# Attention with relative bias, then a max-of-three MoE: transposes moved between the scores and the products with v

## The chip, the cores and the metric

The kernel runs on one core of a Trainium2 chip. The metric is the device time of one execution in microseconds (us); the time of a kernel is the median of several executions. One execution is recorded by the hardware profiler, and all rows of a profile are from that one. The engines of the core are named as in the profile: PE is TensorE (matmuls), PEld its weight loads, DVE is VectorE, ACT is ScalarE, POOL is GpSimd, SP is the engine that issues the DMAs. Each engine carries out its own instructions in the order in which the program issues them; engines wait for one another by semaphores.

## What is computed

The reference, cut to what matters. B = 4, H = 8, S = 576, D = 64; the second part has 2304 tokens, d_model 512, d_ff 768.

```python
scores = scale * np.matmul(q, k.transpose(0, 1, 3, 2))
rel = (pos[:, None] - pos[None, :]).astype(np.float32)
psi_rel = np.log1p(np.abs(rel))
psi_i = np.log1p(np.maximum(pos[:, None].astype(np.float32), 1.0))
x = (psi_rel / psi_i)[..., None]
bias = np.maximum(x @ w1 + b1, 0.0) @ w2
scores = scores + bias.transpose(2, 0, 1)[None, :, :, :]
attn = np.exp(scores - np.max(scores, axis=-1, keepdims=True))
attn = attn / (np.sum(attn, axis=-1, keepdims=True) + 1e-09)
attn_out = np.matmul(attn, v)
x = attn_out.transpose(0, 2, 1, 3).reshape(B * S, H * D)
h = np.maximum(np.maximum(x @ mw1, x @ mw2), x @ mw3)
out = h @ mw_out
```

## The kernel before

The program has three stages. A bias stage builds the bias of all heads and writes it to DRAM. The attention stage works through 16 units; a unit is one batch and two heads, and two units form a pair. The MoE stage follows on the same engines; its weights are converted in small pieces of side work that are threaded into the attention stage.

The order of work is written out by hand (a manual schedule): the program issues everything in the order of the code, and each engine follows it.

A pair takes NS = 9 steps, eight pairs make 72 steps, n = 0 to 71, and four more (72 to 75) empty the pipeline. A step handles 128 rows of scores of both heads of a unit; one step of each pair, y = MIX = 4, takes the last 64 rows of both units together. From the second pair on y = n % 9. In step n the kernel does these things, each for a different stage of the pipeline:

- scores S of step n (`front`, L258): twelve matmuls of 288 columns into two tiles `s`; in the MIX step 16 matmuls at L272. The two `s` buffers are one step's, so the next scores wait for both shifts of this step.
- products P with v (`queue_pv`, L363; matmuls at L385): a finished group of 256 or 320 columns has five products, which wait in the list `pvq`. Step n takes 3, 2, 3, 2, 3, 2, 2, 2 or 1 of them, by n % 9; in the first 18 steps 3, but never across the end of a group. The accumulator `pv` has one buffer. A finished group is copied out by VectorE (`split_x`, L403).
- shift (L283, VectorE L289): scores plus bias, and the row minimum; exponential (`expo`, L295, ScalarE L303) with its row sums; one for each of the two heads.
- normalisation of step n - 2 (`norm`, L309): a reciprocal on VectorE (L313) for every two steps, and a multiplication on GpSimd (L317).
- transposes T of step f = n - 4 (`flip`, L326; transposes at L344): 16 into two tiles `tp` of one bank each, and two into a small tile `lp`. The first transpose of a step writes `lp`. `tp` has two buffers, which one step fills; `lp` has one.
- copies of the transposes into `et`: ScalarE copies one `tp` (L431) and the first part of `lp` (L432), VectorE the other `tp` (L434). In the MIX step `lp` has two parts, for two units; the second is copied by ScalarE at the end of the step (L458). `et` has two buffers, one for each group.

On TensorE a step is S, P, T. On ScalarE it is, as a rule, exponential 0, exponential 1, copies; in steps after which a group is queued or n % 9 = 7 (`ends`) it is exponential 0, copies, exponential 1, and then the rest. On VectorE it is shift 0, shift 1, the copies of finished products, side work (`between`; in `ends` steps it comes last), the reciprocal, the copy of `tp`. A group is queued at the end of the steps n % 9 = 8, 1, 3 and 5, so its products begin in the step after. The transposes of the MIX step (f % 9 = 4) fall into n % 9 = 8.

Of the kernel before, what the change touches and what calls it, by code (L numbers as in the profile page):

```python
# [19 lines left out]
def kernel(  # L20
# [12 lines left out]
    nc = tc.nc  # L33
# [117 lines left out]
    def finish(pool, k, load, g, i, keep):  # L151
        bs = pool.tile([128, S + 16], F32, tag="bs", bufs=12 + KEPT, name=f"bs{g}")
        ip = k["ipo"][:, g:g + 1]
        w = S + 15
        o = bs[:, 0:w]
        if load["act"] + 0.96 * w + 165 <= load["dve"] + 1.04 * w + 185:
            nc.scalar.activation(o, i, ACTF.Copy, scale=ip)
            load["act"] += 0.96 * w + 165
        else:
            nc.vector.tensor_scalar(out=o, in0=i, scalar1=ip, scalar2=None, op0=ALU.mult)  # L160
            load["dve"] += 1.04 * w + 185

        def write(pair=None):

            n, step = (H, 1) if pair is None else (2, H // 2)
            dst = bass.AP(tensor=bias_d.tensor, offset=bias_d.offset + 16 * g * H * BW,
                          ap=[[H * BW + 1, 16], [step * BW, n], [1, S + 15]])
            nc.sync.dma_start(out=dst, in_=bs[::step, 0:S + 15])

        if keep:  # L170
            write(0)
            kept.append(write)
        else:
            write()
# [5 lines left out]
    def load_bias(hp, t):  # L180
        if t < NTQ:
            nc.sync.dma_start(out=bias_t[t], in_=bias_rows(128 * t, 128, hp, 0, S, 2))
        else:
            for p in (0, LEFT):
                nc.sync.dma_start(out=bias_t[t][p:p + LEFT], in_=bias_rows(LB, LEFT, hp, 0, S, 2))
# [11 lines left out]
    NS = len(STEPS)  # L197
# [3 lines left out]
    NSTEP = len(sched)  # L201
# [5 lines left out]
    def step_of(pair, y):  # L207
        return ORDERS[units[2 * pair][0] % 2][y]

    class Attention:  # L210
# [198 lines left out]
        def step(self, n, more=()):  # L409
            m, f = n - BATCH, n - LAG  # L410
            if n < NSTEP:
                pair, y = fronts[n]
                which, t = step_of(pair, y)
                un = 2 * pair + which
                if pair + 1 < PAIRS and y in (0, 5):
                    self.load_qk(2 * pair + 2 + (y == 5))
                if y in (3, 7) and (pair or y == 7):
                    self.load_v(2 * pair + (y == 7))
                self.front(n)
            back = 0 <= f < NSTEP  # L420
            for _ in range((3, 2, 3, 2, 3, 2, 2, 2, 1)[n % NS] if n >= 2 * NS else 3):
                if self.pvq and self.pvq.pop(0)() and n < 2 * NS:
                    break
            done = [(un, g) for at, un, g in ((MIX if fronts[f][0] else 3, 0, 1), (1, 0, 0), (6, 1, 1), (8, 1, 0))
                    if back and fronts[f][1] == at]
            ends = bool(done) or n % NS == 7
            rest = []

            def empty():
                tp0, tp1, left = self.flip(f)  # L430
                nc.scalar.copy(*tp0[0])  # L431
                nc.scalar.copy(*left[0])  # L432
                for x in tp1:
                    nc.vector.tensor_copy(*x)  # L434
                rest.extend(tp0[1:] + left[1:])

            def between():
                for w in more:
                    w.go(False)

            if n < NSTEP:
                for h in range(2):
                    self.shift(n, h)
                    if not (ends and h):
                        self.expo(n, h)
            self.split_x()
            if not ends:
                between()
            if 0 <= m < NSTEP:
                self.norm(m)  # L450
            if back:
                empty()
            if ends:
                if n < NSTEP:
                    self.expo(n, 1)
                between()
            for x in rest:
                nc.scalar.copy(*x)  # L458
            if n < NSTEP and units[2 * pair + 1][1] == border[-1] and which and units[2 * pair][0] + 1 < HP:
                load_bias(units[2 * pair][0] + 1, t)  # L460
            for un, g in done:
                un += 2 * fronts[f][0]
                self.queue_pv(un, g, *self.et[un])
            if n < NSTEP:
                pair, y = fronts[n]
                k = n - (NS * pair + (3 if pair else 6))
                if 0 <= k < 2 and 2 * pair + 2 < len(units):
                    if k == 0:
                        self.splits = self.prep(2 * pair + 2, None if pair else nc.vector)
                    next(self.splits)  # L470
                if pair and y <= 1:
                    if y == 0:
                        self.splits = self.prep(2 * pair + 1)
                    next(self.splits)
            for w in dict.fromkeys(more):
                if w.go(True):
                    break
# [573 lines left out]
    with tc.manual_schedule():  # L1051
# [4 lines left out]
        n = 0  # L1056
# [209 lines left out]
```

## Time and profile before

| | before |
|---|---|
| median of 3 runs | 544.99 us (544.58 to 545.15) |
| the profiled execution | 545.0 us |
| its span, first to last instruction | 543.2 us |
| TensorE busy | 526.1 us (97%), 5209 matmuls |
| VectorE busy | 441.3 us (81%) |
| ScalarE busy | 362.0 us (67%) |
| GpSimd busy | 295.8 us (54%) |
| mean granted TensorE clock | 0.997 |

The attention stage's scores begin at 48 us and its last products end at 272 us of the span. A busy time is the share in which an engine's records cover the time; the ends of matmuls are modelled, so on TensorE the starts are the safer thing to read: from the first matmul of S to the first of P, and so on. A row of the timeline gives the start, the duration of the merged group, engine, line, operation, out<-in with shapes, and in brackets the idle time of the engine ahead of it with its releaser.

### The profile page before, as it was taken

Reading aid. Unit: us, or ns where it says so; the run is one execution under the profiler, and the core shown is the slowest. Engines: PE = TensorE matmul, PEld = TensorE weight load, DVE = VectorE, ACT = ScalarE, POOL = GpSimd, SP = SyncE. Lnnn points to the kernel's source line nnn. Section 1 sums busy time; section 2 is a strip of 40 time slices with the busy share of each in tenths; the row PEclk is TensorE's granted clock in tenths of the full one; section 3 lists DMA queues with packets and bytes.
Section 4 is the critical chain, followed back from the end, with each engine's and each line's share of the span. In section 5 each row is a group of like instructions: output and inputs, shape, how many; then the busy total and the mean of one; then the engine's idle time right before and its main releaser. Section 6 shows DMA issues by size and latency. Waiting matters only on the chain.

```text
span 543.2 us, 13700 instructions
## 1 busy us (share of the span) xinstructions
PE 526.1 (97%) x5209; PEld 435.5 (80%) x5209; DVE 441.3 (81%) x915; ACT 362.0 (67%) x812; POOL 295.8 (54%) x296
## 2 busy tenths in 40 slices
PE   7999889999999999999899999999999999999997
PEld 3455666676766666667599999999999999999997
DVE  7998789999998999888598878767886357798883
ACT  7998899998989898988575542443424325454552
POOL 1957687697898987776500525656476534400000
PEclk9999899999999999999999999999999999999999
DMA  5895985664694166211101234531274520666552
GB/s 168 229 344 151 343 256 171 209 181 127 196 287 136 25 201 189 69 23 24 40 1 62 96 116 150 200 134 43 77 272 155 176 87 0 216 188 193 171 164 79
DMA packets 74034, 80.76 MB, mean 149 GB/s; under 512 B 23216, under 2 KB 54576, under 8 KB 73968
## 3 DMA queue, kind: packets, MB, share of 16 engines
q1 hardware_dynamic: 73824, 79.58, 46.7%
q8 instruction: 41, 0.67, 0.5%
q10 hardware_dynamic: 144, 0.29, 0.2%
q14 instruction: 25, 0.20, 0.1%
HBM read 50.61 MB, written 28.99 MB: 147 GB/s over the span
## 4 chain that ended last, share of the span: by engine, by line
PE 58%; DVE 2%; DMA 1%; ACT 1%; issue 1%; DVEq 0%; ACTq 0%
PE p L607 11%; PE p L605 11%; PE p L606 11%; PE pv L385 5%; PE p_o L977 3%; PE p_o L975 3%; PE p_o L976 3%; PE s L279 3%; PE tp L344 2%; PE c L605 2%; PE c L606 2%; PE c L607 2%; DMA hin<-h_d 1%; PE lp L344 1%; PE s L272 1%
## 5 line engine op out<-in xcount | busy, mean ns | idle before, releaser
L317 POOL TENSOR_SCALAR e<-e,rc 128x576 f32<-128x576 f32 x144 | 113.3, 805 | 31.5 <-DVE rc L313 24.0
L303 ACT ACTIVATE e<-sn,nm 128x576 f32<-128x576 f32 x144 | 111.7, 777 | 16.6 <-DVE nm L289 13.7
L289 DVE CUSTOM_DVE_ANT_0 sn<-s,bias 128x576 f32<-128x576 f32 x144 | 102.9, 752 | 12.1 <-PE s L279 7.6
L385 PE MATMUL pv<-et,vt 128*64 128x320 f32 (+1 forms) x496 | 74.2, 419 | 2.6 <-ACT et L431 2.0
L497 POOL TENSOR_TENSOR wl<-wr,wh 128x256 fp32r<-128x256 f32 x25 | 23.4, 963 | 74.8 <-ACT wh L693 74.8
L434 DVE COPY et<-tp 128x512 f32<-128x512 f32 x72 | 48.9, 679 | 14.4 <-PE tp L344 11.5
L344 PE MATMUL tp<-ident,e 64*128 64x64 f32 x1152 | 55.7, 227 | 0.0
L385 PEld LDWEIGHTS pv<-et,vt 128*64 128x64 f32 x496 | 31.6, 136 | 26.4 <-issue 5.6
L279 PE MATMUL s<-kh,qh 64*128 64x288 f32 x256 | 50.2, 338 | 1.8 <-DVE nm L289 1.4
L244 POOL TENSOR_TENSOR kl<-kr,kh 128x576 fp32r<-128x576 f32 x16 | 41.3, 2583 | 19.3 <-ACT kh L241 18.8
L344 PEld LDWEIGHTS lp<-ident,e 64*128 64x128 f32 x144 | 19.9, 138 | 33.3 <-issue 20.8
L431 ACT COPY et<-tp 128x512 f32<-128x512 f32 x72 | 41.4, 575 | 6.8 <-PE lp L344 6.2
L344 PEld LDWEIGHTS tp<-ident,e 64*128 64x128 f32 x1152 | 45.7, 140 | 0.0
L134 PE MATMUL bp<-hid,w2s 128*32 128x79 f32 (+51 forms) x640 | 41.0, 391 | 3.4 <-DVE hid L113 3.1
L279 PE MATMUL s<-kl,qh 64*128 64x288 f32 x256 | 43.3, 297 | 0.0
L279 PE MATMUL s<-kh,ql 64*128 64x288 f32 x256 | 42.3, 293 | 0.1
L113 DVE TENSOR_SCALAR hid<-sm,bp 128x528 f32<-128x528 f32 (+17 forms) x108 | 40.5, 454 | 0.0
L134 PEld LDWEIGHTS bp<-hid,w2s 128*32 128x32 f32 x640 | 20.4, 109 | 24.5 <-issue 15.7
L344 PE MATMUL lp<-ident,e 64*128 64x64 f32 x144 | 35.6, 248 | 2.8 <-ACT et L432 1.3
L497 POOL TENSOR_TENSOR wl<-ws,wh 128x256 fp32r<-128x256 f32 x28 | 29.4, 1074 | 14.3 <-ACT wh L695 14.3
L652 ACT COPY u<-p 128x384 f32<-128x384 f32 x24 | 11.5, 480 | 37.0 <-PE p L607 37.0
L279 PEld LDWEIGHTS s<-kh,qh 64*128 64x128 f32 x256 | 30.0, 189 | 4.8 <-DVE nm L289 3.8
(231 smaller groups left out, 1620.2 us busy)
## 6 DMA issues: line engine op xcount, KB each, us to landing
bias_d<-bs SPq DMA_DIRECT2D x36, 295.5 KB, 5.4
bias<-bias_d SPq DMA_DIRECT2D x16, 576.0 KB, 6.0
w<-in_moe_w_dram SPq DMA_DIRECT2D x36, 256.0 KB, 3.2
h_d<-ht SPq DMA_DIRECT2D x18, 384.0 KB, 3.4
hin<-h_d SPq DMA_DIRECT2D x16, 384.0 KB, 4.6
qr<-in_qd_dram SPq DMA_DIRECT2D x16, 288.0 KB, 5.1
kr<-in_kd_dram SPq DMA_DIRECT2D x16, 288.0 KB, 5.5
vt<-in_v_dram SPq DMA_DIRECT2D x32, 128.0 KB, 3.3
```

Source lines behind the costliest of these rows:

```text
L134: nc.tensor.matmul(bp[32 * c:32 * c + 32, o:o + w], lhsT=w2s, rhs=src, start=True, stop=True)
L279: nc.tensor.matmul(ss[h][:, x, 0:HALF], lhsT=u[q][p, 128 * t:128 * t + 128], rhs=u[k][p, cols], start=(j == 0), stop=(j == 2))
L289: nc.vector.tensor_tensor_reduce(out=sn.rearrange("p (a b) -> p a b", a=2), in0=st["s"][h][:, :, 0:HALF], in1=bt.rearrange("p (a b) -> p a ...
L303: nc.scalar.activation(st["e"][:, S * h:S * h + S], sn, ACTF.Exp, scale=-1.0, bias=nm, accum_out=self.sm[:, x:x + 1])
L317: nc.gpsimd.tensor_scalar(out=e, in0=e, scalar1=self.rc[:, x:x + 1], scalar2=1.0, op0=ALU.mult, op1=ALU.mult)
L344: return nc.tensor.transpose(to, e2[p, k0:k0 + 128], ident[p, p])
L385: nc.tensor.matmul(pv[p], lhsT=w, rhs=x, start=(c == 0), stop=(c == NTQ))
L434: nc.vector.tensor_copy(*x)
L497: eng.tensor_tensor(out=out, in0=f(a), in1=f(b), op=op)
L605: nc.tensor.matmul(o, lhsT=hi[:, c], rhs=h[:, j], start=first and j == 0, stop=False, **on)
L606: nc.tensor.matmul(o, lhsT=hi[:, c], rhs=l[:, j], start=False, stop=False, **on)
L607: nc.tensor.matmul(o, lhsT=lo[:, c], rhs=h[:, j], start=False, stop=last and j == 1, **on)
```

## The change

From n = 9 on, except in steps with n % 9 = 8, a step is "turned". In a turned step the copies of finished products (`split_x`) stand at its head, the transposes follow the scores, and the products follow the transposes. ScalarE is issued the copies of the transposes (all parts of `lp` with them) ahead of the exponentials. VectorE is issued the shifts, then the copy of its `tp`, then the reciprocal, then the side work. The four steps after the last scores are turned too. The first nine steps and those with n % 9 = 8 stay in the old order.

```diff
+                turned = n >= NS and n % NS != NS - 1
+                if turned:
+                    self.split_x()
                 self.front(n)
+            else:
+                turned = True
+                self.split_x()
             back = 0 <= f < NSTEP
-            for _ in range((3, 2, 3, 2, 3, 2, 2, 2, 1)[n % NS] if n >= 2 * NS else 3):
-                if self.pvq and self.pvq.pop(0)() and n < 2 * NS:
-                    break
+
+            def products():
+                for _ in range((3, 2, 3, 2, 3, 2, 2, 2, 1)[n % NS] if n >= 2 * NS else 3):
+                    if self.pvq and self.pvq.pop(0)() and n < 2 * NS:
+                        break
+
+            if not turned:
+                products()
...
             def empty():
                 tp0, tp1, left = self.flip(f)
-                nc.scalar.copy(*tp0[0])
-                nc.scalar.copy(*left[0])
+                soon = len(left) if turned else 1
+                for x in tp0 + left[:soon]:
+                    nc.scalar.copy(*x)
+                if turned:
+                    products()
+                    if n < NSTEP:
+                        for h in range(2):
+                            self.shift(n, h)
                 for x in tp1:
                     nc.vector.tensor_copy(*x)
-                rest.extend(tp0[1:] + left[1:])
+                rest.extend(left[soon:])
...
-            if n < NSTEP:
+            if turned:
+                if back:
+                    empty()
+                else:
+                    products()
+                for h in range(2 if n < NSTEP else 0):
+                    self.expo(n, h)
+                if 0 <= m < NSTEP:
+                    self.norm(m)
+                between()
+            else:
                 for h in range(2):
                     self.shift(n, h)
                     if not (ends and h):
                         self.expo(n, h)
-            self.split_x()
-            if not ends:
-                between()
-            if 0 <= m < NSTEP:
-                self.norm(m)
-            if back:
-                empty()
-            if ends:
-                if n < NSTEP:
+                self.split_x()
+                if not ends:
+                    between()
+                if 0 <= m < NSTEP:
+                    self.norm(m)
+                if back:
+                    empty()
+                if ends:
                     self.expo(n, 1)
-                between()
-            for x in rest:
-                nc.scalar.copy(*x)
+                    between()
+                for x in rest:
+                    nc.scalar.copy(*x)
```

## Rows read from the trace of the kernel before

**Rows 1.** Busy time by engine in one pair's stretch (PE, PEld, DVE, ACT, POOL).

```profile
205.00:232.00 27.00, 26.78 (x354) 18.19 (x354) 24.38 (x64) 24.56 (x66) 19.92 (x24) 1.00 0.38 115
```

**Rows 2.** Timeline, TensorE, step 54 to the scores of step 55.

```profile
204.43 0.40 PE L279 MATMUL s<-kh,qh 64*128 64x288 f32 x1
205.11 0.40 PE L279 MATMUL s<-kh,qh 64*128 64x288 f32 x1 [0.28 <-DVE nm L289]
...
206.10 1.84 PE L385 MATMUL pv<-et,vt 128*64 128x320 f32 x12
...
207.87 0.77 PE L344 MATMUL tp<-ident,e 64*128 64x64 f32 x16
...
208.44 0.38 PE L279 MATMUL s<-kh,qh 64*128 64x288 f32 x2
```

**Rows 3.** Timeline, ScalarE and VectorE, the same stretch.

```profile
204.47 0.78 ACT L303 ACTIVATE e<-sn,nm 128x576 f32<-128x576 f32 x1 [0.63 <-DVE nm L289]
...
205.38 0.67 DVE L434 COPY et<-tp 128x512 f32<-128x512 f32 x1
...
205.82 0.78 ACT L303 ACTIVATE e<-sn,nm 128x576 f32<-128x576 f32 x1
...
206.83 0.19 ACT L458 COPY et<-lp 128x64 f32<-128x64 f32 x1
```

**Rows 4.** Timeline, ScalarE and TensorE, step 8: second copy of `lp`, next transpose.

```profile
69.06 0.19 ACT L458 COPY et<-lp 128x64 f32<-128x64 f32 x1
...
69.39 0.24 PE L344 MATMUL lp<-ident,e 64*128 64x64 f32 x1 [1.01 <-ACT et L458]
```

**Rows 5.** Timeline, steps 18 and 63: first product, second copy of `lp`.

```profile
98.05 1.83 PE L385 MATMUL pv<-et,vt 128*64 128x320 f32 x12
...
98.85 0.20 ACT L458 COPY et<-lp 128x64 f32<-128x64 f32 x1
...
233.17 1.83 PE L385 MATMUL pv<-et,vt 128*64 128x320 f32 x12
...
233.66 0.21 ACT L458 COPY et<-lp 128x64 f32<-128x64 f32 x1
```

**Rows 6.** Timeline, TensorE, step 55 and step 72: products and transposes.

```profile
209.41 0.76 PE L385 MATMUL pv<-et,vt 128*64 128x320 f32 x4
...
210.64 0.27 PE L344 MATMUL lp<-ident,e 64*128 64x64 f32 x1
...
260.82 0.27 PE L344 MATMUL lp<-ident,e 64*128 64x64 f32 x1
...
261.52 0.76 PE L385 MATMUL pv<-et,vt 128*64 128x320 f32 x4
```

**Rows 7.** Timeline, TensorE, step 58 (n % 9 = 4): mixed scores, then products.

```profile
217.43 1.76 PE L272 MATMUL s<-kr,qr 64*64 64x288 f32 x16
...
217.89 0.78 PEld L272 LDWEIGHTS s<-kr,qr 64*64 64x64 f32 x14 [0.28 <-DVE nm L289]
...
219.12 0.41 PEld L385 LDWEIGHTS pv<-et,vt 128*64 128x64 f32 x6 [0.44 <-ACT et L432]
```

**Rows 8.** Timeline, steps 72 to 75: products and the second copy of `lp`.

```profile
259.05 1.84 PE L385 MATMUL pv<-et,vt 128*64 128x320 f32 x12 [0.88 <-ACT et L431]
...
260.02 0.20 ACT L458 COPY et<-lp 128x64 f32<-128x64 f32 x1
...
264.30 1.84 PE L385 MATMUL pv<-et,vt 128*64 128x320 f32 x12 [0.77 <-ACT et L431]
...
269.59 1.95 PE L385 MATMUL pvlast<-et,vt 128*64 128x256 f32 x16 [0.82 <-ACT et L432]
```

**Rows 9.** Timeline, TensorE, step 61: scores, then products.

```profile
226.35 0.78 PE L279 MATMUL s<-kh,qh 64*128 64x288 f32 x2
...
227.71 0.44 PE L385 MATMUL pv<-et,vt 128*64 128x256 f32 x2
```

**Rows 10.** Timeline, GpSimd, steps 57 and 58: normalisations, four merged.

```profile
216.11 2.91 POOL L317 TENSOR_SCALAR e<-e,rc 128x576 f32<-128x576 f32 x4 [0.83 <-DVE rc L313]
```

## Prediction

> **What bounds the kernel now.** I read first the busy shares of one stretch as long as a pair of units, then the order of time on TensorE, then on ScalarE and VectorE in the same stretch, and last who released whom. In 27 us TensorE is busy for 26.78, VectorE for 24.38, ScalarE for 24.56 [rows 1]: TensorE sets the pace of the attention stage, the others are some 10% behind. So the change can win only what TensorE waits for, and loses whatever new wait it puts in front of TensorE.
>
> One step of TensorE before is scores S, products P, transposes T. Prices by starts: S to P 0.97 (208.44 to 209.41), two products of 320 columns 1.23, three 1.76, T to the next S 0.58 [rows 2, 6]. Only T directly ahead of P stands at 0.70 (260.82 to 261.52) [rows 6], in the four steps after the last scores.
>
> The regular wait is in the first step of every pair (n % 9 = 0). Its scores start at 204.43, their second half only at 205.11, released by VectorE's shift; P starts at 206.10 [rows 2]. There are six such steps from step 18 to 63. The other regular one is n % 9 = 4 (raw scores of both units' last 64 rows): there P's weight load was idle 0.44 until ScalarE's copy of `lp` [rows 7].
>
> **The change, part by part.** No instruction is added or removed; only orders move. From n = 9 on, except n % 9 = 8, TensorE does S, T, P; ScalarE does both its copies of the transposes (`tp`, `lp`) ahead of the two exponentials; VectorE does the copies of finished products at the head of the step, then shifts, its `tp` copy, the reciprocal, the side work.
>
> *Switching on TensorE.* Before, a step holds S to P (0.97), P to T, T to S (0.58). After, it holds S to T, T to P (0.70), P to S. S to T and P to S are not shown without a wait. The shapes in the rows tell which neighbours resemble each other: S and T are both 64\*128, P is 128\*64 [rows 2]. T to S costs nothing visible (207.87 to 208.44 [rows 2], 18 transposes), so I take S to T as free too: S then lasts 0.97 less the 0.12 to 0.15 by which T to P exceeds T to S, 0.82 to 0.85, and P to S costs what P to T costs. Sum: 0.83 + 0.70 against 0.97 + 0.58, so 0 within 0.02 a step. The other end, S to T as dear as S to P, is 0.12 to 0.15 in each of 55 steps, 7 to 8 us; the row of T to S is the nearest, so I take 0. (The Trainium skill, TensorEngine Tiling (Array Packing), Key Properties, says that a change of the tiling mode, not of the tile, drains the engine; by it S to T is free and the two changes a step stay two, the sum is 0; the 0.70 against 0.58 in rows 6 agrees with it.)
>
> *The step after the one that keeps the old order (n % 9 = 0).* This is the term that decides. `lp` has one buffer. In step n % 9 = 8 the transposed step is the mixed one, with two copies out of `lp`; only the first is made at once, the second (line 458) stands last on ScalarE, behind the second exponential: the first exponential starts at 204.47, the second at 205.82, the L458 copy at 206.83, when the scores of the next step are 2.4 us old [rows 2, 3]. Before, T of that next step is behind S and three products and starts at 207.87, a full us later, so nobody waits. After, T stands directly behind S, its first transpose writes `lp`, and the products are queued behind it on TensorE. That T really waits for L458 is shown once: L458 starts at 69.06, the first transpose starts at 69.39, idle 1.01 until L458 [rows 4]. So T starts at L458 + 0.33, P at L458 + 0.33 + 0.70; before, P started at its own time and T cost 0.58 behind it. Loss a step = L458 start - P start + 0.45.
> Step 54: 206.83 - 206.10 + 0.45 = 1.18. Step 18: 98.85 - 98.05 + 0.45 = 1.25; step 63: 233.66 - 233.17 + 0.45 = 0.94 [rows 2, 3, 5]. The other three (27, 36, 45) give 0.93, 1.19, 1.17 in the same way. Six steps: 6.7 us. L458 can't come sooner: its ScalarE chain begins with VectorE's shift of step 8, which step 8 does as before. What waits behind: the products, then the next scores, and on ScalarE the exponentials of this step, which now stand behind the `tp` copy.
>
> *The steps after the last scores.* Step 71 is also n % 9 = 8, with L458 at 260.02; P started at 259.05 [rows 8]. After: T at 260.35, P at 261.05. From there, three products 1.76, T 0.70, two 1.23, T 0.70, three 1.76, T 0.70, two 1.07 (with no T behind them): 7.9, so the last products start at 269.0 against 269.59. The waits of 0.77 and 0.82 for ScalarE's copies [rows 8] are covered by T and P now in between. Gain 0.6.
>
> *n % 9 = 4.* T comes between the mixed scores and P, and the copies it needs lead ScalarE. The wait of 0.44, less some 0.16 that a change of shape leaves anyway, goes: 0.28; the rest of that step's delay is the shift (weights released at 217.89 [rows 7]) and stays. Of seven such steps five show it: gain 1.2, bounds 0 and 2.
>
> *Small waits elsewhere.* The largest lets 1.36 pass between S and P instead of 0.97 [rows 9]; some 15 of 0.06 to 0.39 sum to 3.2. They come from VectorE being late with a shift because of side work. VectorE's `tp` copy no longer waits for T behind three products, but the side work itself stays in front of the next shift. I take 1.0 gained, bounds 0 and 3.2.
>
> *GpSimd's normalisation.* T moves ahead by the length of P, so e must be normalised sooner; and the reciprocal falls behind VectorE's `tp` copy (0.61 to 0.67 [rows 3]), though ahead of the side work. For step 58 GpSimd begins at 216.11 with four, so the two that T needs end at 217.57 [rows 10]; T would start at 217.43 + 1.0 [rows 7], 0.8 later. Cover holds by about the delay; cost 0, bound 0.2 in each of some 14 tight steps, 3 us.
>
> *The first nine turned steps.* There the products are still cut in other portions (three, then the rest of a group), and a group's `et` buffer comes free only with the products of the same step, which now stand behind T. The copies of steps 11, 13 and 15 wait for them, and T of the next step for the copies: some 0.1 each beyond cover. Steps 9 and 10 give about 0.2 back. Net cost 0.2, bounds -0.5 and 1.
>
> Sum: 6.7 - 0.6 - 1.2 - 1.0 + 0.2 = +4.1. The profiled execution of before took 545.0 (span 543.2 and 1.8 around it), the median of the runs shown is 544.99, so nothing has to be rescaled: 549.1. After the attention stage TensorE is full, so the delay comes through to the end.
>
> **The rivals.**
> *Faster: T is not held by L458.* If the second small copy were no condition of the first transpose, or came sooner, T would wait for the big copies only: VectorE's begins at 205.38 and lasts 0.67 [rows 3], so P at 206.05 + 0.70 = 206.75 against 206.10, less 0.58: +0.07 a step, 0.4 in six, and the tail gains 2. Sum 0.4 - 2 - 1.2 - 1.0 + 0.2 = -3.6: 541.4. The wait in rows 4 and the copy's fixed place on ScalarE speak against it. Chance 0.09. (The Trainium skill, Perfetto Trace Analysis, Matmuls, asks that independent groups rotate through PSUM banks so that evacuation overlaps the next group; `lp` doesn't rotate, so by it the wait is there. Rows 4 agree.)
> *No change: the loss is given back.* The extra us a pair lets VectorE and ScalarE catch up, and all waits of the pair's other steps (1.2 + 0.8 of n % 9 = 4 beyond it, 3.2 small) vanish: 6.7 - 0.6 - 2 - 3.2 + 0.2 = +1.1, or with P to S cheaper by 0.02 a step 0: 545 to 546.1. Against it: side work is fixed in the order and hits VectorE after the shifts of a later step. Chance 0.12.
> *Much slower: the unseen switch or a late GpSimd.* S to T costs 0.12 in 55 steps, or T waits 0.2 for e: +3 to +7 on top: 552 to 556. T to S at 0.58 speaks against it. Chance 0.09.
>
> **How the numbers follow.** Forecast as summed, 547 to 551.3, chance 0.70. About 0.2% (1.1 us) is what a measurement of this kernel can tell from no change. The range takes in the no-change case's upper part: 545.4 to 551.6. Faster by over 0.2%: 0.10; within: 0.13; slower: 0.77.
>
> **What would show it.** In the profile after, in steps 18, 27, 36, 45, 54, 63 and 72: weight loads of `lp` idle over 1 us until ScalarE's L458 (its line will differ), T 2.2 to 3.0 after its scores, the next scores 4.5 to 5.4 after them (before 3.4 to 4.3). Waits of P for `et` gone. T in the other turned steps 0.8 to 0.9 behind S. I am wrong if T in n % 9 = 0 starts within 1.8 of its scores, if the idle time before it names GpSimd or VectorE, or if S to T stands near 0.97 in ordinary steps.

## The result and the profile after

The change makes the kernel slower: 551.16 us median (550.08 to 551.49, 4 runs) beside 545.07 (544.58 to 545.18, 4 runs) of before, a ratio of 1.011 with a 95% interval of 1.0093 to 1.0128. On another chip the same two kernels took 551.40 (5 runs) and 546.22 (15 runs), ratio 1.0099 [1.0085, 1.0112]. The profiled execution of after took 550.08, span 548.3, mean granted clock 0.999. The forecast was 549.1, range 545.4 to 551.6.

The time from the scores of one step to the next scores is read off the starts in the timeline of TensorE. These stretches add up to the difference of the two profiled executions:

| stretch | before | after | difference |
|---|---|---|---|
| start of the span to the scores of step 9 | 69.95 | 69.72 | -0.2 |
| steps 9 to 17 | 27.07 | 29.70 | +2.6 |
| steps 18 to 70 | 158.70 | 161.84 | +3.1 |
| scores of step 71 to the first MoE matmul | 16.18 | 15.76 | -0.4 |
| MoE stage | 271.3 | 271.3 | 0.0 |

The third stretch hardly varies: three more profiles of kernels with the same steps there (e2, e9 and e10 below) gave 161.82 to 161.89, and another in the old order (e4) 158.69. By kind of step (n % 9), before to after: the six of 0 together +5.7; those of 4 -1.2; those of 3 -0.9; those of 6 -0.6; those of 2 +0.3; the rest -0.2.

The first rows are those that answer [rows 1 to 3]: the busy times of a pair's stretch (the columns of [rows 1]), then step 54 on TensorE, then on ScalarE. The line numbers have moved: L444 is ScalarE's copies at the transposes (L431, L432 before), L451 is VectorE's (L434), L484 the second copy of `lp` (L458), L572 to L582 the conversions of weights, the side work. All rows are of after.

```profile
205.00:232.00 27.00, 25.91 (x355) 18.16 (x355) 22.85 (x62) 24.66 (x66) 21.80 (x24) 1.00 0.54 163
```

```profile
209.30 0.74 PE L279 MATMUL s<-kh,qh 64*128 64x288 f32 x2
...
211.70 0.24 PE L344 MATMUL lp<-ident,e 64*128 64x64 f32 x1 [1.00 <-ACT et L484]
...
212.40 1.84 PE L385 MATMUL pv<-et,vt 128*64 128x320 f32 x12
214.17 0.40 PE L279 MATMUL s<-kh,qh 64*128 64x288 f32 x2
...
215.06 0.21 PE L344 MATMUL lp<-ident,e 64*128 64x64 f32 x1
...
215.71 0.76 PE L385 MATMUL pv<-et,vt 128*64 128x320 f32 x4
...
216.94 0.40 PE L279 MATMUL s<-kh,qh 64*128 64x288 f32 x2
```

```profile
209.00 0.78 ACT L303 ACTIVATE e<-sn,nm 128x576 f32<-128x576 f32 x1 [0.24 <-DVE nm L289]
...
209.78 0.57 ACT L444 COPY et<-tp 128x512 f32<-128x512 f32 x1
210.24 0.21 ACT L444 COPY et<-lp 128x64 f32<-128x64 f32 x1
210.35 0.78 ACT L303 ACTIVATE e<-sn,nm 128x576 f32<-128x576 f32 x1
...
211.36 0.19 ACT L484 COPY et<-lp 128x64 f32<-128x64 f32 x1
```

In a pair's stretch TensorE is now busy 25.91 of 27 us where it was 26.78. The wait stands in step 54, between scores and transposes: the scores end at 210.7, the second copy of `lp` starts at 211.36 behind the second exponential, and the first transpose starts 0.34 later, at 211.70. The products follow at 212.40, three us behind the scores; before it was 1.67 [rows 2]. The step after it (scores at 214.17) is an ordinary one: transposes at +0.89, products 0.65 behind them, next scores 1.23 behind those.

One row must not be taken at its word. The weight load of that transpose names GpSimd, the matmul names ScalarE; GpSimd's own timeline decides.

```profile
211.67 0.13 PEld L344 LDWEIGHTS lp<-ident,e 64*128 64x128 f32 x1 [1.21 <-POOL e L317]
```

```profile
207.96 1.47 POOL L317 TENSOR_SCALAR e<-e,rc 128x576 f32<-128x576 f32 x2 [0.63 <-DVE rc L313]
```

GpSimd had normalised both tiles of that step by 209.43, 2.3 us before the transpose; the copy of L484 ended at 211.55.

What TensorE waited for from 60 to 280 us (the view of waits: line, releaser, total us, times, longest), after:

```profile
PE lp L344 <- ACT et L484: 7.8, 7, 2.2
PE lp L344 <- POOL e L317: 2.2, 2, 1.2
PE pv L385 <- PE lp L344: 1.3, 3, 0.7
PE lp L344 <- ACT et L444: 1.3, 2, 1.0
PE s L279 <- DVE nm L289: 0.9, 4, 0.3
```

Seven waits for L484, 7.8 us: step 8, which before has too [rows 4]; steps 18, 27, 45, 54 and 63; and the longest, 2.2, step 72. Step 36 stands in the second line, by its row on TensorE, with GpSimd's rows behind it:

```profile
156.59 0.24 PE L344 MATMUL lp<-ident,e 64*128 64x64 f32 x1 [1.01 <-POOL e L317]
```

```profile
152.82 1.48 POOL L317 TENSOR_SCALAR e<-e,rc 128x576 f32<-128x576 f32 x2 [2.74 <-DVE rc L313]
155.78 1.46 POOL L317 TENSOR_SCALAR e<-e,rc 128x576 f32<-128x576 f32 x2
```

Step 36 transposes what step 32 computed. Counted from the start of the program, the pair of multiplications at 152.82 is that of step 32, and it ended at 154.30, 2.3 us before the transpose; the pair at 155.78 belongs to the next step's transposes. L484 starts at 156.25, and the transpose 0.34 later, as in step 54. In all seven steps from 18 to 72 the first transpose starts 0.33 to 0.35 behind the start of L484, and GpSimd had ended the tiles of the step at least 1.7 us before it. The third line of the waits, products that wait although the engine named is TensorE itself, is the second finding (below). None of its five lines has products waiting for a copy into `et`, which [rows 8] showed for before.

### The profile page after: what moved, and what is told of

Read it like the earlier page. It is cut to its first block, busy times and chain, and to the rows that moved or that the text cites. A ratio compares the mean times of both kernels' runs of the same rounds, so it can differ in the third digit from the quotient of the medians.

```text
span 548.3 us, 13699 instructions
## 1 busy us (share of the span) xinstructions
PE 525.0 (96%) x5209; PEld 438.4 (80%) x5209; DVE 434.9 (79%) x915; ACT 360.8 (66%) x812; POOL 287.5 (52%) x296
## 4 chain that ended last, share of the span: by engine, by line
PE 82%; ACT 8%; DVE 4%; issue 2%; DMA 2%; POOL 1%; DVEq 0%; ACTq 0%; POOLq 0%
PE pv L385 13%; PE p L631 10%; PE p L633 10%; PE p L632 10%; PE s L279 8%; PE bp L134 7%; PE tp L344 5%; ACT e L303 4%; PE p_o L1003 3%; PE p_o L1001 3%; PE p_o L1002 3%; PE s L272 2%; PE c L631 2%; PE c L632 2%; PE c L633 2%
## 5 line engine op out<-in xcount | busy, mean ns | idle before, releaser
L451 DVE COPY et<-tp 128x512 f32<-128x512 f32 x72 | 49.2, 684 | 9.3 <-PE tp L344 4.1
L444 ACT COPY et<-tp 128x512 f32<-128x512 f32 x72 | 41.8, 580 | 21.4 <-PE lp L344 17.5
L344 PE MATMUL tp<-ident,e 64*128 64x64 f32 x1152 | 52.7, 224 | 0.0
L244 POOL TENSOR_TENSOR kl<-kr,kh 128x576 fp32r<-128x576 f32 x16 | 35.9, 2244 | 23.9 <-ACT kh L241 23.4
L344 PEld LDWEIGHTS tp<-ident,e 64*128 64x128 f32 x1152 | 47.1, 139 | 0.0
L134 PE MATMUL bp<-hid,w2s 128*32 128x79 f32 (+51 forms) x640 | 42.5, 411 | 2.8 <-DVE hid L113 1.8
L344 PE MATMUL lp<-ident,e 64*128 64x64 f32 x144 | 33.0, 229 | 11.9 <-ACT et L484 7.8
L134 PEld LDWEIGHTS bp<-hid,w2s 128*32 128x32 f32 x640 | 21.9, 115 | 24.0 <-issue 14.3
```

Source lines behind the costliest of these rows:

```text
L134: nc.tensor.matmul(bp[32 * c:32 * c + 32, o:o + w], lhsT=w2s, rhs=src, start=True, stop=True)
L344: return nc.tensor.transpose(to, e2[p, k0:k0 + 128], ident[p, p])
```

## The experiments

Three groups of kernels, each with the kernel before on the same chip; its medians there are 546.03, 545.90 and 546.22 us. Every edit is to the changed kernel unless it is said otherwise. The columns on the right are read from each kernel's one profiled execution.

| run | median us (runs) | ratio to before [95%] | steps 9 to 17 | 18 to 70 | 71 to MoE |
|---|---|---|---|---|---|
| e1_lp_early | 545.91 (12) | 1.0000 [0.9984, 1.0017] | 28.69 | 158.19 | 14.79 |
| e2_from18 | 550.71 (6) | 1.0091 [1.0069, 1.0112] | 26.85 | 161.89 | 17.34 |
| e3_both | 544.29 (10) | 0.9959 [0.9944, 0.9974] | 28.11 | 158.09 | 14.80 |
| e4_before_lp_early | 546.34 (12) | 0.9999 [0.9984, 1.0014] | 28.20 | 158.69 | 16.19 |
| e5_step0_old | 546.56 (10) | 1.0018 [0.9992, 1.0044] | 28.88 | 157.42 | 17.16 |
| e6_copies_last | 569.84 (4) | 1.0437 [1.0396, 1.0478] | 30.66 | 178.07 | 15.75 |
| e7_split_first | 543.28 (12) | 0.9951 [0.9933, 0.9969] | 27.50 | 157.25 | 14.78 |
| e8_all_turned | 543.03 (12) | 0.9947 [0.9923, 0.9972] | 28.83 | 157.25 | 14.26 |
| e9_after_again | 551.40 (5) | 1.0099 [1.0085, 1.0112] | 28.97 | 161.82 | 17.30 |
| e10_from18_again | 550.05 (5) | 1.0077 [1.0058, 1.0096] | 28.24 | 161.87 | 15.77 |
| e11_split_from9 | 543.28 (5) | 0.9946 [0.9926, 0.9966] | 29.26 | 157.25 | 14.78 |
| e12_split_again | 544.19 (11) | 0.9961 [0.9944, 0.9977] | 27.48 | 157.28 | 14.78 |

### Is it the second copy of `lp`?

e1_lp_early: in the step that keeps the old order, ScalarE copies the second part of `lp` right behind the first, ahead of the second exponential.

```diff
-                soon = len(left) if turned else 1
+                soon = len(left)
```

> The changed kernel, and in the steps n % 9 = 8 the second copy out of lp stands right behind the first, ahead of the second exponential. Theory (T of the next step waits for that copy): T at n % 9 = 0 then waits only for the big copies and starts some 1.7 us after its scores instead of 2.2 to 2.6; 0.7 to 0.8 us in each of six steps and 1.1 us in the steps after the last scores come back, 5.5 us: 545.6 us, and no idle time of TensorE names this copy any more. Rival (the copy is only the last name on a wait that the turned order makes anyway, by T ahead of P and exponentials behind copies): within 0.2% of the changed kernel, 551 us.

e4_before_lp_early is its control, the same edit to the kernel before (line 432):

```diff
-                nc.scalar.copy(*left[0])
+                for x in left:
+                    nc.scalar.copy(*x)
```

> The kernel before, with only the second copy out of lp moved ahead of the second exponential. Theory (in the old order T starts a full us after that copy, nobody waits): 545.0 us, no change within 0.2%. Rival (the late copy already cost something, and any gain of the first experiment is this gain): 543 to 544 us.

e5_step0_old leaves the copy where it is and puts the steps with n % 9 = 0 back into the old order:

```diff
-                turned = n >= NS and n % NS != NS - 1
+                turned = n >= NS and 0 < n % NS < NS - 1
```

> The changed kernel with the steps n % 9 = 0 left in the old order too, the late second copy out of lp unchanged. Theory (only T of that step meets the late copy): the step goes from 4.9 us back to 3.9, six times 5.7 us; the next step's T, turned, then meets copies of an old-order step, made behind the exponentials, and loses some 0.3 us each time: 547 us, and TensorE doesn't wait for L458's successor in steps 18 to 63. Rival (any change of order between neighbouring steps costs such a wait): 549 to 551 us.

e1, step 54 on TensorE and ScalarE:

```profile
204.89 0.74 PE L279 MATMUL s<-kh,qh 64*128 64x288 f32 x2
...
206.31 0.24 PE L344 MATMUL lp<-ident,e 64*128 64x64 f32 x1
...
207.01 1.83 PE L385 MATMUL pv<-et,vt 128*64 128x320 f32 x12
...
208.78 0.40 PE L279 MATMUL s<-kh,qh 64*128 64x288 f32 x2
```

```profile
205.84 0.32 ACT L444 COPY et<-lp 128x64 f32<-128x64 f32 x2
206.05 0.79 ACT L303 ACTIVATE e<-sn,nm 128x576 f32<-128x576 f32 x1
```

With both small copies at 205.84 the transposes start 1.42 behind the scores where after has 2.40, and the step takes 3.89 instead of 4.87. All of it goes: 18 to 70 is 3.65 shorter than in after, the tail 0.97, the time is that of before. In before the same edit changes nothing (158.69, 16.19): there nobody waits for that copy. e5 removes the wait in the six steps by the other end and 18 to 70 falls by 4.4; the step behind it then lasts 3.07 instead of 2.77, and the wait in the tail, which this edit doesn't touch, stays. By kind of step, in e1 those of n % 9 = 0 fall by 5.2 in all against after, and those of 2 rise by 1.5, which e7 takes up. So one copy out of a tile with one buffer carries the loss of the stage; the turned order without it is worth 0.5 us there and 1.4 in the tail, less than the 3.6 that the prediction's rival had put on it.

### The first nine turned steps

e2_from18 begins to turn at step 18, and e3_both has both edits.

```diff
-                turned = n >= NS and n % NS != NS - 1
+                turned = n >= 2 * NS and n % NS != NS - 1
```

> The changed kernel, turned from n = 18 on instead of n = 9. Theory (in the first turned pair the copies of T wait for the et buffer, that is for products that now stand behind T, and the next accumulator waits behind them): the stretch from the scores of step 9 to those of step 18 goes from 29.7 us back to 27.1, of which 1.1 us are waits for et and the accumulator and 1.5 us a wait of ScalarE for a weight's DMA that may or may not be there; 548.5 to 550 us. Rival (the long first pair was an accident of one execution): 551 us.

> Both edits: second copy out of lp early, and turned from n = 18 on. Theory (two separate causes, one behind the other on TensorE): the gains add up, 5.5 and 1.1 to 2.6: 543 to 544.6 us, slightly below the kernel before, since n % 9 = 4 and 3 gain some 2 us. Rival (the turned order itself is dearer than the old one): not below 547 us.

e3 is 1.6 us below e1 on the same chip, but e2, at 550.71, is hardly below after. The columns tell why: its first pair is 2 to 3 us shorter, its tail 1.6 longer, with the same instructions there; the tail has a section below. Where the first pair loses shows on TensorE, VectorE and ScalarE in steps 11 and 12 of after:

```profile
78.34 0.24 PE L344 MATMUL lp<-ident,e 64*128 64x64 f32 x1 [1.23 <-POOL e L317]
...
82.70 1.57 PE L385 MATMUL pv<-et,vt 128*64 128x320 f32 x10 [0.66 <-PE lp L344]
```

```profile
80.42 0.69 DVE L451 COPY et<-tp 128x512 f32<-128x512 f32 x1 [0.54 <-PE pv L385]
81.03 1.05 DVE L576 TENSOR_SCALAR wa<-wa 128x512 uint32<-128x512 uint32 x1
82.00 0.61 DVE L405 COPY xb<-pv 128x128 f32<-128x128 f32 x3
```

```profile
76.89 0.67 ACT L572 ACTIVATE wa<-w 128x512 f32<-128x512 f32 x1 [1.58 <-DMA vt<-in_v_dram]
77.46 0.57 ACT L444 COPY et<-tp 128x512 f32<-128x512 f32 x1
77.93 0.27 ACT L444 COPY et<-lp 128x128 f32<-128x128 f32 x1
```

Read VectorE's rows downwards. Its copy into `et` waits 0.54 for the products of the step, because a group's buffer comes free only with them. The side work (L576) follows in its fixed place, and the copy of the finished products (L405, `split_x`) stands at the head of the next step, behind that. `pv` has one buffer, so the products of step 12 wait for L405: idle 0.66. The same in step 16 (0.36). Steps 12 and 16 together take 6.71 in before and 7.77 in after. ScalarE's rows are another matter: a conversion of weights (L572) waits 1.58 for a transfer, the copies behind it are late, and the transposes of step 11 with them. The row names the transfer of `vt`, which the conversion doesn't read; its input `w` was issued just ahead of that transfer, and e10's row of the same wait (1.57) names `w`. This wait comes and goes: step 11 lasts 4.22 here, 3.48 in e9 with a wait of 0.82, 2.78 in e1 with none, 2.77 in before, and 3.45 in e10, where the first pair has the old order. So the wait isn't the change's doing, but in these single profiles it costs more in the turned order: 1.44 of 1.58 in after, 0.67 of 1.57 in e10.

e7_split_first tests the accumulator's part: e3 with the copies of finished products ahead of the side work of the same step.

```diff
                 if 0 <= m < NSTEP:
                     self.norm(m)
+                self.split_x()
                 between()
```

> The third experiment's kernel (late copy early, turned from n = 18), and VectorE copies finished products ahead of the side work of the step instead of behind it. Theory (products of a new group wait for the accumulator, whose copy stands behind side work; seen as 0.2 to 0.95 us in step n % 9 = 2 of four pairs): these steps fall from 3.5 to 4.25 us to 3.31, 2.1 us in all: 542.2 us. Rival (the side work is then late instead, and with it the next shift and scores): 544.3 us, no change from the third experiment.

Step n % 9 = 2 of a later pair, in e3 and in e7; first TensorE and VectorE of e3, then of e7:

```profile
158.15 0.22 PE L344 MATMUL lp<-ident,e 64*128 64x64 f32 x1
159.24 1.84 PE L385 MATMUL pv<-et,vt 128*64 128x320 f32 x12 [0.87 <-PE tp L344]
```

```profile
157.03 1.58 DVE L579 SCALAR_TENSOR_TENSOR wa<-w,wa 128x512 uint32<-128x512 uint32 x1
158.53 0.61 DVE L405 COPY xb<-pv 128x192 f32<-128x192 f32 x3
```

```profile
158.15 0.22 PE L344 MATMUL lp<-ident,e 64*128 64x64 f32 x1
158.31 1.84 PE L385 MATMUL pv<-et,vt 128*64 128x320 f32 x12
```

```profile
157.17 0.61 DVE L405 COPY xb<-pv 128x192 f32<-128x192 f32 x3
157.69 0.92 DVE L580 SCALAR_TENSOR_TENSOR wa<-w,wa 128x512 uint32<-128x512 uint32 x1
```

The wait of 0.87 is gone, and the six steps of that kind fall from 3.66 to 3.32 each. A part comes back: two steps with n % 9 = 4 take 3.72 and 4.05 instead of 3.28 and 3.75, and one with 3 takes 3.22, since VectorE's side work now ends later before the next shift. The stage gains 0.84 by the traces, not the 2.1 of the six steps. The times don't resolve it: on three chips the ratios to before are 0.9959 (e3), 0.9951 (e7) and 0.9961 (e12).

e9_after_again and e10_from18_again are after and e2 once more, side by side; e12_split_again is e7, and e11_split_from9 is e7 turned from step 9.

> The changed kernel itself, beside the version that is turned only from step 18. Theory A (the first nine turned steps cost 1.3 to 2.6 us, whatever the tail does): the changed kernel is 1.3 to 2.6 us above the version from 18. Theory B (the place of the loss is a matter of the bias stage's execution, and both have the same tail): no more than 0.5 us between them.

> Turned from step 18 only, everything else as in the changed kernel. Theory A: 1.3 to 2.6 us below the changed kernel, first pair near 27 us. Theory B: within 0.5 us of it, because what the first pair wins is lost where TensorE's clock falls after the idle time of 2.2 us in the tail; then the stretch after that idle time shows a granted clock below 0.9, in the changed kernel 1.0.

> Turned from step 9, with the second small copy right behind the first, and the copies of finished products ahead of the side work instead of behind it. If the first turned pair loses because its first products wait for an accumulator that VectorE empties behind side work (idle 0.66 and 0.36 in steps 12 and 16), the cost against the same kernel turned from 18 falls from 1.6 to some 0.6 us. If it loses because the group buffer comes free later and ScalarE waits for a weight transfer, the cost stays at 1.3 us or more.

> The same kernel turned from 18, for the comparison with the one turned from 9: first pair near 27 to 28 us, 543.3 in all.

The changed kernel is 1.35 us above the version from 18, at the lower end of theory A; in steps 12 and 16 the two profiles have 7.77 against 6.89. The time is a rough measure here, since the tail's clock falls in some executions of either (below). In these two profiles theory B's sign stands the other way round: the clock fell in the tail of the changed kernel (17.30 us) and held in that of e10 (15.77), whose first pair took 28.24, not 27. With `split_x` ahead of the side work the loss isn't there: steps 12 and 16 take 6.61 in e11 and 6.70 in e12. Steps 13 and 14, which wait for `et` alone, take 6.21 in all five profiles turned from step 9 with the copies in front (after, e1, e5, e9, e11) and 5.93 to 6.57 in the eight old ones, no cost beyond that spread. The times, 543.28 and 544.19 with overlapping runs (541.26 to 544.82 and 543.05 to 545.92), show no cost. By the first pair as a whole (29.26 against 27.48) the second reading of e11's expectation would stand. But step 10 alone makes 1.45 of that, 5.45 us long at a granted clock of 0.69; e8 has such a step (5.59, also 0.69) with the first pair in the old order. The other eight steps differ by 0.3. So the accumulator behind side work is the cause in steps 12 and 16, about 1 us. The first pair varies by more than that without the change (26.85 to 28.83 in the eight profiles with the old order); what of it was traced is the wait for a transfer in step 11 and the clock in step 10.

### The order of the copies, and the step left out

e6_copies_last keeps TensorE's new order, but puts the exponentials of turned steps ahead of the copies on ScalarE.

```diff
-                for x in tp0 + left[:soon]:
-                    nc.scalar.copy(*x)
                 if turned:
                     products()
                     if n < NSTEP:
                         for h in range(2):
                             self.shift(n, h)
+                            self.expo(n, h)
+                for x in tp0 + left[:soon]:
+                    nc.scalar.copy(*x)
...
-                for h in range(2 if n < NSTEP else 0):
-                    self.expo(n, h)
```

> The changed kernel with one half of the change undone: in turned steps ScalarE does both exponentials ahead of its copies, TensorE keeps S, T, P. Theory (T of the next step needs tp and lp free, and ScalarE's copies end some 4.2 us after the scores behind two exponentials): T waits in every step of two products, 0.3 to 0.4 us in five steps of nine, some 11 us in all: 560 to 563 us, with idle time of TensorE ahead of lp named by ScalarE's copies. Rival (the place of the copies on ScalarE is free, the other engines have slack): 551 us.

It is 24 us above before and some 18 above the changed kernel (ratios 1.0437 and 1.0110), where 9 to 12 above the changed kernel were expected. The view of waits from 60 to 280 us, e6, TensorE (L450 the copies, L483 the second copy of `lp`):

```profile
PE lp L344 <- ACT et L450: 14.7, 25, 1.1
PE lp L344 <- ACT et L483: 5.7, 6, 1.1
```

Transposes wait for the copies 25 times, where after had two such waits. The lead of the copies on ScalarE is the other half of the change: without it transposes directly behind the scores wait in every pair.

e8_all_turned is e7 with step n % 9 = 8 turned too.

```diff
-                turned = n >= 2 * NS and n % NS != NS - 1
+                turned = n >= 2 * NS
```

> The seventh experiment's kernel with the steps n % 9 = 8 turned as well. Theory (what is left at n % 9 = 0 is T waiting for the copies of an old-order step; turned, step 8 has its T 0.6 us earlier and its copies ahead of the exponentials, and they need only the one product that stands behind T): T at n % 9 = 0 starts 0.9 to 1.0 us behind its scores' last wait, step 0 falls by 0.3 to 0.7 us, 2 to 3 us in all: 539.5 to 540.5 us. Rival (the copies of the mixed step wait for the group buffer, whose last product now stands behind T, and T of the next step waits for them): 543 to 546 us.

The steps of n % 9 = 0 fall from 4.01 to 3.80 and the tail from 14.78 to 14.26, but a mixed step (49) then waits 1.2 for a shift behind side work, and 18 to 70 is as long as in e7. The time is the one that the rival gave, by another wait than the one it named; e7 and e8 can't be told apart by time. Both beat before, by 0.5% (the intervals above): the turned order is a gain when its two new waits are taken out.

### The tail and the clock

After and e9 are the same kernel. The windows of its tail (columns as in [rows 1]: PE, PEld, DVE, ACT, POOL, granted clock, DMA, GB/s), first after, then e9:

```profile
266.00:268.00 2.00, 2.00 (x28) 1.34 (x30) 0.77 (x2) 1.28 (x3) 0.38 (x1) 1.00 0.41 162
268.00:270.00 2.00, 2.00 (x30) 1.12 (x26) 0.69 (x1) 0.99 (x4) 2.00 (x4) 1.00 0.00 0
```

```profile
266.00:268.00 2.00, 2.00 (x16) 1.02 (x13) 0.78 (x2) 1.49 (x3) 0.92 (x2) 0.69 0.09 35
268.00:270.00 2.00, 2.00 (x22) 1.04 (x18) 0.00 (x0) 0.00 (x0) 2.00 (x4) 0.50 0.00 0
```

TensorE of after, then of e9, behind the wait of step 72:

```profile
265.93 0.24 PE L344 MATMUL lp<-ident,e 64*128 64x64 f32 x1 [2.18 <-ACT et L484]
...
266.63 1.84 PE L385 MATMUL pv<-et,vt 128*64 128x320 f32 x12
268.40 0.27 PE L344 MATMUL lp<-ident,e 64*128 64x64 f32 x1
```

```profile
265.39 0.24 PE L344 MATMUL lp<-ident,e 64*128 64x64 f32 x1 [2.19 <-ACT et L484]
...
266.09 2.88 PE L385 MATMUL pv<-et,vt 128*64 128x320 f32 x12
268.90 0.36 PE L344 MATMUL lp<-ident,e 64*128 64x64 f32 x1
```

Both waited 2.2 us. In after the three products then took 1.84 at a clock of 1.00; in e9 the same products took 2.88, and the granted clock was 0.50 from 268 to 270, the lower of its two levels (1.2 GHz). The tail is 1.5 us longer for it. Six profiles have that wait of 2.2 us in step 72 (after, e2, e5, e6, e9, e10). In three of them, e2, e5 and e9, the granted clock falls to 0.50 during the wait or within 1.4 us behind it (tails of 17.16 to 17.34); in the other three it stays at 1.00 (15.75 to 15.77). None of the eight profiles without the wait shows the low clock in the tail. So the idle time makes the drop likely, by this count, and does not bring it each time; no run forced it. It isn't needed for one either: the steps 10 of e8 and e11 have the low clock with no wait of TensorE over 0.4 us since the scores of step 9.

## Why the prediction was right, and where its sum was wrong

The direction and the mechanism that decides were right, and 549.1 lay 2.1 below the median: one term was too large, one too small, one was missing, and one had its size for a wrong reason.

- *The bound.* TensorE sets the pace: the differences of the stretches, read off its starts, add up to the 5.1 us between the two profiled executions, and the MoE stage behind takes 271.3 in both, so the delay comes through to the end.
- *n % 9 = 0, summed 6.7, measured 5.7.* The mechanism holds in each part: transposes start 0.34 behind L484 (0.33 assumed), products 0.70 behind them, the step takes 4.64 to 5.07 (4.5 to 5.4 given). Steps 18 and 27 lost 1.26 and 0.95 (1.25 and 0.93 given); step 54 lost 0.86 where the sum had 1.18. The step that failed is "L458 can't come sooner": it starts 2.06 behind the scores of step 54 in after (209.30 to 211.36) and 2.40 in [rows 3]. ScalarE's chain in the step of n % 9 = 8 does begin with VectorE's shift, but that shift came sooner against the scores: the first exponential starts 0.30 ahead of the scores of step 54 in after, 0.04 behind them in [rows 2, 3]. Why the shift was sooner no run tested.
- *n % 9 = 4, summed -1.2, measured -1.2: the number was right by luck.* (Five steps at 0.28 are 1.4 besides.) The sum took the 0.44 ahead of P's weight load for a wait for ScalarE's copy of `lp`. In step 58 that copy ran from 218.50 for 0.27 and had ended 0.35 before the weight load [rows 7], and the same 0.44 stands where nothing was late: in before's step 67, first below, where S to P is 1.13, and in after ahead of the transposes' weight load of step 58, where S to T is 1.13.

```profile
244.61 1.20 PE L272 MATMUL s<-kr,qr 64*64 64x288 f32 x16
245.74 1.06 PEld L385 LDWEIGHTS pv<-et,vt 128*64 128x64 f32 x12 [0.44 <-ACT et L432]
```

```profile
224.31 0.13 PEld L344 LDWEIGHTS lp<-ident,e 64*128 64x128 f32 x1 [0.44 <-POOL e L317]
```

What went is the part that the prediction let stand, the wait of the mixed scores for VectorE's shift [rows 7]. In before the mixed scores stood behind T and started ahead of the end of the last shift; in after they stand behind the products, and S to the next matmul falls in four steps, from between 1.62 and 1.96 to 1.13 in three of them and 1.58 in one. These four steps gained 1.5; the two that had no such wait lost 0.14 each, since T to P is dearer than T to S.

- *Small waits, -1.0 against -1.4*, within the bounds. Some 0.7 of the 1.4 is no wait: in before T to the mixed scores took 0.70 at the end of each step of n % 9 = 3, where T to other scores takes 0.58, and now products stand there. In the rest n % 9 = 2 lost 0.3 to the accumulator, which no term had.
- *Switching, 0 against 0.* S to T, T to P and P to S are 0.89, 0.65 and 1.23: 2.77 with two products, where before had 2.78. The bound of 7 to 8 us for a dear S to T is gone. (The Trainium skill, TensorEngine Tiling (Array Packing), Key Properties, has the drain at a change of mode and not of tile; S to T at 0.89 instead of 0.97 agrees, and the sum over a step doesn't change, as two changes remain.)
- *GpSimd, 0 against 0.* From step 18 on its name stands at one transpose, step 36, whose tiles it had ended 2.3 us before; in no step from 18 on did it end less than 1.1 us ahead of the first transpose.
- *The tail, -0.6 against -0.4* where the clock held. In three profiles of six it fell and the tail got 1.0 to 1.2 longer than before's, a price that the prediction didn't have. Whether that is why the median lies 1.1 above the profiled execution (mean granted clock 0.999) stays open: two of the other three runs had 0.993, but the slowest, 551.49, had 1.000.
- *The first nine turned steps, summed +0.2 with an upper bound of 1: the mis-sized term.* Measured were 2.6 in the profiled execution. The prediction saw that copies wait for `et` until the products are done, and priced what lies directly behind, 0.1 a step; steps 13 and 14 took 6.21 where before had 6.11. It did not follow VectorE's queue one place further: side work, then `split_x`, then TensorE again by the one `pv`. That was 1.1 us (6.71 to 7.77), and e11 shows that it goes when `split_x` changes places with the side work. The other part of the 2.6, 1.45 in step 11, is the wait for a transfer, which falls into either order and cost more in the turned one. The 0.2 that steps 9 and 10 were to give back were 0.02.

The sum came within 1.0 of the 5.1 between the profiled executions because the term of n % 9 = 0 (1.0 too high) and that of the first nine steps (2.4 too low) erred in opposite directions, which is in part luck. The signs to look for were right but for one: the idle time names GpSimd at weight loads and at the transpose of step 36, by which the prediction would have called itself wrong. The timelines of GpSimd and ScalarE put it right.

Of the rivals, "faster" came out in e1 for the wait and in e3 for the time: without L484 there is no loss. It promised 3.6 us, and e3 gained 1.7 against before on its chip: the rival knew nothing of the accumulator (0.84, e7) and had the tail's gain at 2.0 (measured 1.4). "No change" failed on the price of L484, "much slower" on the switch.

## What to carry to other kernels

When work on an in-order engine is moved forward, look up every reader of the buffer that it writes, and where the last of them stands in its own queue: here a copy of 0.2 us, harmless for the old order, held the busiest engine 1.0 us in each of six steps, and moving it gave all back. Then follow the queue of each engine that the new order makes wait past the waiting instruction: what stands behind it (here side work, then the copy that frees a single accumulator) is late too, and the loss appears one step on. A wait on the engine that sets the end may also cost clock behind it, here some 1.5 us in three of six profiles, and a forecast should name that. And a name in a bracket is no proof of a cause: check when the engine named had ended, and whether the same idle time stands in a step where nothing was late.

## What the runs showed of the hardware

- The same wait of 2.2 us on TensorE, in the same kernel, was followed in one execution by a granted clock of 1.00 and in another of 0.69 and 0.50 over 2 us each; three products took 1.84 and 2.88, the stretch to the MoE stage 15.76 and 17.30. Of six profiles with the wait three had the low clock.
- Two neighbouring changes of shape differ in price by their order: transposes to products 0.65 to 0.70, transposes to scores 0.58 [rows 2, 6], scores to transposes 0.89 where scores to products is 0.97 [rows 2, 6]. Over a step with two products the differences cancel, 2.77 against 2.78.
